# Retention followed by a feed-forward block: the later token blocks in units of 256 tokens by 4 heads, and state products as 64x64 TensorE tiles

## The chip, the cores and the metric

The kernel runs on one core of one Trainium2 chip. The metric is the device time of one execution in microseconds (us). One execution was profiled; its trace gives the start and duration of every instruction.

## The reference

Retention with a decay per head, then a two-layer feed-forward block with PReLU; all inputs and the output are float32.

```python
# q, k, v: (4, 8, 768, 64); w_in: (512, 2048); w_out: (2048, 512); alpha: (2048,)
gamma = 1.0 - 2.0 ** (-5.0 - np.arange(H))          # per head
for t in range(S):
    state = gamma[None, :, None, None] * state + np.einsum('bhd,bhe->bhde', k[:, :, t], v[:, :, t])
    y[:, :, t] = (1 / sqrt(D)) * np.einsum('bhd,bhde->bhe', q[:, :, t], state)
x = y.transpose(0, 2, 1, 3).reshape(B * S, H * D)   # (3072, 512)
h = x @ w_in
out = (np.maximum(h, 0) + alpha * np.minimum(h, 0)) @ w_out
```

## The kernel before

The 3072 tokens are six blocks of 512. A block is four units, and unit `u` runs through the same steps:

- **Load**: k, q and v come from memory through SP's queue (`load`, lines 131 and 139).
- **Scale**: k and q are multiplied by powers of gamma from a table `tab` and rounded to float16 (`kdq`; `prep` line 157 or `u_scale` line 289), v is rounded (`vx`). In blocks 2 to 5 GpSimd (POOL) does all three; in blocks 0 and 1 VectorE (DVE) does k.
- **Turn**: `kdq` is transposed into `kq`, by TensorE and a ScalarE (ACT) copy in blocks 0 and 1 (`u_turn`), by a DMA transpose on SP's queue later (line 165).
- **State**: k times v per pair of heads (`stp`), added to the carried state on VectorE (`ss`), multiplied by the decay on GpSimd (`tg`). A sequence is six chunks of 128 tokens, and the last one needs no new state.
- **Scores**: k times q (`sca`, `scb`), masked on VectorE into `m2`.
- **Output**: `yps` gathers the carried state times q and the masked scores times v; ScalarE copies it into `xT`, the input of the feed-forward block.

There are two forms of unit. Blocks 0 and 1 (units 0 to 7, functions with `u_`) take 256 tokens by 4 heads: two units share the tokens and halve the heads. Partition `p` holds two neighbouring tokens, so a load reads runs of 512 bytes. Its products use one row half of TensorE for the first 128 tokens and the other for the next (`hf`). Blocks 2 to 5 (units 8 to 23: `prep`, `stage_a`, `stage_b`, `stage_c`) take 128 tokens by 8 heads, with runs of 256 bytes.

The trace writes a product's tile shape as rows*columns of the TensorE array: `128*128` is the whole array, `64*64` one of four tiles. In blocks 2 to 5 the state (L199) and the carried product (L248) are 128*128, the product with v (L258) 128*64, the scores (L223) 64*128. In blocks 0 and 1 the state (L341) is 64*128, the scores (L381) and the product with v (L415) are 64*64, the carried product (L427) 128*128.

The feed-forward block is `ffn1(n)` (16 groups of 4 wide products, L460; ScalarE computes `hm` at L470 and VectorE `gt` at L471 from each) and `ffn2(n)` (64 wide products, L500; ScalarE copies `os` at L509 and issues the store itself at L513). Both are generators. `tick(gen, m)` issues the next `m` wide products, and the schedule written out by hand puts the short products of the next block between them. I call such an insertion a visit. In blocks 2 to 5 there are five per block: four within `ffn2` that start a unit and (from the second on) put out the one before, and a last one that only puts out.

All PSUM tiles share eight banks under one tag (`ps`). Every engine takes its instructions in the order in which the program issues them, so the hand-written order decides what waits behind what: on SP the loads and the transposes, on ScalarE the copies and the stores, on GpSimd the scaling, the decay products and the issue of the weight loads (`get_wi`, `get_wo`). The first load of unit 8 is held until the last quarter of `w_out` has arrived (`held`).

Of the kernel before, what the change touches and what calls it, by code (L numbers as in the profile page):

```python
# [10 lines left out]
F16 = mybir.dt.float16  # L11
# [7 lines left out]
def kernel(  # L19
# [10 lines left out]
    nc = tc.nc  # L30
# [16 lines left out]
    NTAB = 6 * H + NP + 16  # L47
    TU = 2 * H + NP
    tab_np = np.zeros((128, NTAB), dtype=np.float64)
    for h in range(H):  # L50
        tab_np[:, h] = g64[h] ** (127.0 - p_ar)
        tab_np[:, H + h] = scale * g64[h] ** (p_ar + 1.0 - 128.0)
    for p in range(NP):
        tab_np[0:64, 2 * H + p] = g64[2 * p] ** 128
        tab_np[64:128, 2 * H + p] = g64[2 * p + 1] ** 128
    for s in range(2):
        loc = 2.0 * (p_ar % 64) + s
        for h in range(H):
            tab_np[:, TU + H * s + h] = g64[h] ** (127.0 - loc)
            tab_np[:, TU + 2 * H + H * s + h] = scale * g64[h] ** (loc + 1.0 - 128.0)  # L60
    tab_np[0:NFT, NTAB - 16 : NTAB] = np.eye(NFT)
    tab_np = tab_np.astype(np.float32)
    mi_np = np.zeros((128, 512), dtype=np.float16)
    mi_np[:, 0:128] = p_ar[:, None] <= p_ar[None, :]
    mi_np[:, 128:256] = np.eye(128)
    half_ar = np.arange(64)
    for s in range(2):
        for t in range(2):
            keep_np = (2 * half_ar[:, None] + s) <= (2 * half_ar[None, :] + t)
            c0 = 256 + 128 * s + 64 * t  # L70
            mi_np[0:64, c0 : c0 + 64] = keep_np
            mi_np[64:128, c0 : c0 + 64] = keep_np
# [9 lines left out]
    mi = sbp.tile([128, 512], F16, tag="mi", name="mi")  # L82
    mask = mi[:, 0:128]
    ident = mi[:, 128:256]
    masku = mi[:, 256:512].rearrange("p (s i) -> p s i", s=2)
# [8 lines left out]

    NV = 8
    NPE = 8
    NUN = 8
    vext = [sbp.tile([128, NP, 3, 64], F16, tag=f"vx{i}", name=f"vx{i}") for i in range(NV)]

# [21 lines left out]
    def load(u, names="kqv"):  # L121
        b, c = divmod(u, NCH)
        t = staged.setdefault(u, {})
        for nm in names:
            src = srcs[nm]
            st = sbp.tile([128, H * D], FP, tag=f"{nm}s", bufs=8, name=f"{nm}s{u}")
            if u < NUN:
                j, g = divmod(u, 2)
                b, c = divmod(2 * j, NCH)
                t[nm] = st.rearrange("p (h s d) -> p s h d", s=2, d=D)  # L130
                ins = nc.sync.dma_start(  # L131
                    out=st.rearrange("p (h x) -> p h x", h=H // 2),
                    in_=src[
                        b, H // 2 * g : H // 2 * g + H // 2, C * c : C * c + 2 * C, :
                    ].rearrange("h (p s) d -> p h (s d)", s=2),
                )
            else:
                t[nm] = st.rearrange("p (h d) -> p h d", d=D)
                ins = nc.sync.dma_start(  # L139
                    out=t[nm],  # L140
                    in_=src[b, :, C * c : C * c + C, :].rearrange("h p d -> p h d"),
                )
# [10 lines left out]
    def prep(u):  # L153
        t = staged.pop(u)
        kdq = sbp.tile([128, 2, H, D], F16, tag="kdq", bufs=8, name=f"kdq{u}")
        for a, nm in enumerate("kq"):
            nc.gpsimd.tensor_tensor(  # L157
                out=kdq[:, a],
                in0=t[nm],
                in1=tab[:, H * a : H * a + H].unsqueeze(2).to_broadcast([128, H, D]),  # L160
                op=MULT,
            )
        kq = sbp.tile([128, 2 * NP, 128], F16, tag="kq", bufs=8, name=f"kq{u}")
        if u >= NPE:
            nc.sync.dma_start_transpose(
                out=kq, in_=kdq.rearrange("p a h d -> p (a h d)")
            )
        vx = vext[u % NV]
        nc.gpsimd.tensor_copy(  # L169
            out=vx[:, :, 0::2, :],  # L170
            in_=t["v"].rearrange("p (a b) d -> p a b d", b=2),
        )
        prepped[u] = (kdq, kq, vx)


# [3 lines left out]
    def stage_a(u):  # L179
        b, c = divmod(u, NCH)  # L180
        kdq, kq, vx = prepped.pop(u)
        kd = kdq[:, 0]
        if u < NPE:
            trb = ps("trb", F16, 1024)
            for p in range(2 * NP):
                nc.tensor.transpose(
                    out=trb[:, 128 * p : 128 * p + 128],
                    in_=kdq[:, p // NP, 2 * (p % NP) : 2 * (p % NP) + 2, :].rearrange(
                        "p a d -> p (a d)"
                    ),  # L190
                    identity=ident,
                )
            nc.scalar.activation(
                out=kq.rearrange("p a i -> p (a i)"), in_=trb, func=COPY, bias=0.0, scale=1.0
            )
        if c < NCH - 1:
            stp = ps("stp")
            for p in range(NP):
                nc.tensor.matmul(  # L199
                    out=stp[:, 128 * p : 128 * p + 128],  # L200
                    lhsT=kd[:, 2 * p : 2 * p + 2, :].rearrange("p a d -> p (a d)"),
                    rhs=vx[:, p, 0::2, :],
                    start=True,
                    stop=True,
                )
            new = sst[u % NT]
            stv = stp.rearrange("p (a e) -> p a e", e=128)
            tg = sbp.tile([128, NP, 128], F16, tag="tg", bufs=4, name=f"tg{u}")
            if c > 0:
                nc.vector.tensor_tensor(out=new, in0=tgs[u], in1=stv, op=ADD)  # L210
                nc.gpsimd.tensor_tensor(out=tg, in0=new, in1=gmat, op=MULT)  # L211
            else:
                nc.vector.tensor_tensor(out=tg, in0=stv, in1=gmat, op=MULT)
            tgs[u + 1] = tg
        live[u] = (kq.rearrange("p a i -> p (a i)"), vx)

    def stage_b(u):
        kq, vx = live[u]
        scs = [ps("sca"), ps("scb")]
        for p in range(NP):  # L220
            for lh in range(2):
                s = slice(64 * lh, 64 * lh + 64)
                nc.tensor.matmul(  # L223
                    out=scs[lh][:, 128 * p : 128 * p + 128],
                    lhsT=kq[s, 128 * p : 128 * p + 128],
                    rhs=kq[s, 512 + 128 * p : 512 + 128 * p + 128],
                    start=True,
                    stop=True,
                )
        m2s = []  # L230
        for lh in range(2):
            m2 = sbp.tile([128, NP, 128], F16, tag=f"m2{lh}", bufs=2, name=f"m2{lh}")
            nc.vector.tensor_tensor(  # L233
                out=m2,
                in0=scs[lh].rearrange("p (a i) -> p a i", i=128),
                in1=mask.unsqueeze(1).to_broadcast([128, NP, 128]),
                op=MULT,
            )
            m2s.append(m2)
        live[u] = (kq, vx, m2s)  # L240

    def stage_c(u):
        b, c = divmod(u, NCH)
        kq, vx, m2s = live.pop(u)
        yps = ps("yps")
        if c > 0:
            for p in range(NP):
                nc.tensor.matmul(  # L248
                    out=yps[:, 128 * p : 128 * p + 128],
                    lhsT=tgs[u][:, p, :],  # L250
                    rhs=kq[:, 512 + 128 * p : 512 + 128 * p + 128],
                    start=(p == 0),
                    stop=False,
                    skip_group_check=True,
                )
        for p in range(NP):
            for lh in range(2):
                nc.tensor.matmul(  # L258
                    out=yps[64 * lh : 64 * lh + 64, 128 * p : 128 * p + 128],
                    lhsT=vx[:, p, 2 * lh, :],  # L260
                    rhs=m2s[lh][:, p, :],
                    start=(c == 0 and p == 0),
                    stop=(p == NP - 1),
                    skip_group_check=True,
                )
        n, i = divmod(u, UB)
        if i == 0:
            xT[n] = sbp.tile([128, NP, TB], F16, tag="xT", bufs=2, name=f"xT{n}")
        nc.scalar.activation(  # L269
            out=xT[n][:, :, C * i : C * i + C],  # L270
            in_=yps.rearrange("p (a i) -> p a i", i=128),
            func=COPY,
            bias=0.0,
            scale=1.0,
        )


    def u_scale(i, a):
        if i not in prepped:
            kdq = sbp.tile([128, 2, H, D], F16, tag="kdq", bufs=8, name=f"kdq{i}")  # L280
            kq = sbp.tile([128, 2 * NP, 128], F16, tag="kq", bufs=8, name=f"kq{i}")
            prepped[i] = (
                kdq.rearrange("p a (s h) d -> p a s h d", s=2),
                kq,
                vext[i % NV].rearrange("p (s r) x d -> p s r x d", s=2),
            )
# [459 lines left out]
```

## Time and profile before

| | |
|---|---|
| Time, median of 3 runs (lowest to highest) | 221.58 us (221.4 to 223.0) |
| The profiled execution's own time | 221.09 us |
| Its span, first to last instruction | 219.3 us |
| Mean granted TensorE clock | 0.997 of full speed |
| TensorE busy / VectorE / ScalarE / GpSimd | 96% / 55% / 45% / 37% of the span |
| First product of `ffn1(1)`; start of its unbroken run | 56.42 us; 57.97 us |
| `ffn2` of blocks 1, 2, 3, 4 of the loop (visits for blocks 2 to 5) | from 71.5, 104.4, 136.8 and 169.0 us |
| DMA packets under 512 bytes | 67888 of 87507 |

The busy share of TensorE counts overlapping products and is no measure of its peak; the starts of its products tell more. The groups of instructions and the timeline give the line, the engine, the operation, the tile names and the shapes. `PEld` is TensorE's weight load, `SPq` and `ACTq` are the time in which SP's and ScalarE's queues issue a DMA. An entry such as `[0.30 <-DMA kq<-kdq]` is idle time ahead of an instruction and what ended it.

### The profile page before, as it was taken

What the parts mean: (1) busy time and instruction counts of PE and PEld (TensorE: products, weight loads), DVE (VectorE), ACT (ScalarE), POOL (GpSimd) and SP (SyncE); (2) the same over time, 40 slices, a digit from 0 to 9 for tenths busy, and PEclk for the clock granted to TensorE, in tenths of its full rate; (3) what the DMA queues carried; (4) which work ended last, traced back from release to release, by engine and by line L of the source; (5) the groups of instructions that cost most, each with busy time, mean ns of one, the idle gap of its engine ahead of it and who ended that gap; (6) DMA issues with size and microseconds to landing.
All of it is one profiled execution on the core that took longest, in us unless ns stands there. A gap on an engine that the chain in (4) does not pass through costs nothing.

```text
span 219.3 us, 4001 instructions
## 1 busy us (share of the span) xinstructions
PE 209.6 (96%) x1575; PEld 103.8 (47%) x1575; DVE 121.1 (55%) x190; ACT 98.5 (45%) x169; POOL 81.5 (37%) x96
## 2 busy tenths in 40 slices
PE   7899998999899999999999999999999999999992
PEld 3456543454444554444555444555444555444440
DVE  4684896554039953188753288653388742388000
ACT  2583873334359422467232476222576222566121
POOL 3487208731963249900044960205950420000000
PEclk9999999999999999999999999999999999999998
DMA  6999999958999999999911699912640102100111
GB/s 184 300 218 189 193 261 298 218 98 199 259 262 218 216 229 210 236 242 228 200 48 53 173 244 221 223 50 96 146 96 0 44 20 82 48 3 0 48 73 72
DMA packets 87507, 33.99 MB, mean 155 GB/s; under 512 B 67888, under 2 KB 84416, under 8 KB 87488
## 3 DMA queue, kind: packets, MB, share of 16 engines
q1 hardware_dynamic: 79488, 23.08, 47.4%
q0 software_dynamic: 4224, 4.19, 12.2%
q10 hardware_dynamic: 3776, 6.47, 8.0%
q8 instruction: 12, 0.20, 0.4%
q14 instruction: 7, 0.06, 0.1%
HBM read 27.44 MB, written 6.29 MB: 154 GB/s over the span
## 4 chain that ended last, share of the span: by engine, by line
PE 71%; DMA 16%; SPq 6%; POOL 2%; ACT 2%; DVE 1%; issue 1%; ACTq 0%; DVEq 0%
PE hps L460 31%; PE ops L500 31%; DMA vs<-in_v_dram 5%; SPq L131 5%; DMA qs<-in_q_dram 5%; DMA win<-in_moe_w_in_dram 3%; DMA kq<-kdq 2%; PE yps L258 2%; PE sca L223 2%; PE stp L199 1%; SPq L139 1%; PE yps L248 1%; POOL tg L364 1%; ACT kq L322 1%; DVE m L394 1%
## 5 line engine op out<-in xcount | busy, mean ns | idle before, releaser
L471 DVE SCALAR_TENSOR_TENSOR gt<-hm,oma,hps 128x512 f16<-128x512 f32 x96 | 69.3, 745 | 41.2 <-ACT hm L470 34.3
L500 PE MATMUL ops<-wout,gt 128*128 128x512 f16 x384 | 89.4, 380 | 0.0
L460 PE MATMUL hps<-xT,win 128*128 128x512 f16 (+1 forms) x404 | 84.5, 368 | 1.3 <-ACT xT L440 1.3
L470 ACT ACTIVATE hm<-hps 128x512 f32<-128x512 f32 x96 | 56.7, 597 | 22.2 <-PE hps L460 21.0
L460 PEld LDWEIGHTS <-win 128*128 128x128 f16 x404 | 39.3, 97 | 45.0 <-issue 1.8
L500 PEld LDWEIGHTS <-gt 128*128 128x128 f16 x384 | 35.1, 98 | 40.6
L211 POOL TENSOR_TENSOR tg<-ss,gmat 128x512 f16<-128x512 f32 x11 | 14.0, 1270 | 66.6 <-DVE ss L210 66.6
L509 ACT ACTIVATE os<-ops 128x512 f32<-128x512 f32 x24 | 14.3, 598 | 39.3 <-PE ops L500 31.5
L269 ACT ACTIVATE xT<-yps 128x512 f16<-128x512 f32 x16 | 9.6, 597 | 32.3 <-PE yps L258 30.9
L157 POOL TENSOR_TENSOR kdq<-ks,tab 128x512 f16<-128x512 f32 x16 | 16.8, 1049 | 1.8 <-DMA ks<-in_k_dram 1.8
L157 POOL TENSOR_TENSOR kdq<-qs,tab 128x512 f16<-128x512 f32 x16 | 16.8, 1049 | 0.8 <-DMA qs<-in_q_dram 0.8
L322 ACT ACTIVATE kq<-trb 128x512 f16<-128x512 f16 (+1 forms) x11 | 8.7, 790 | 16.0 <-PE trb L313 15.9
L233 DVE TENSOR_TENSOR m<-sca,mi 128x512 f16<-128x512 f32 x16 | 11.0, 690 | 8.6 <-PE scb L223 7.9
L210 DVE TENSOR_TENSOR ss<-tg,stp 128x512 f32<-128x512 f16 x11 | 7.5, 686 | 13.2 <-PE stp L199 13.0
L289 POOL TENSOR_TENSOR kdq<-qs,tab 128x512 f16<-128x512 f32 x8 | 8.3, 1039 | 17.3 <-DMA qs<-in_q_dram 17.3
L233 DVE TENSOR_TENSOR m<-scb,mi 128x512 f16<-128x512 f32 x16 | 10.9, 681 | 0.0
L364 POOL TENSOR_TENSOR tg<-ss,gmat 128x256 f16<-128x256 f32 x10 | 7.7, 777 | 8.3 <-DVE ss L363 8.3
L169 POOL CAST vx<-vs 128x512 f16<-128x512 f32 x16 | 9.9, 616 | 0.3 <-ACT hm L470 0.3
L111 PE MATMUL kps<-spin 128*128 128x512 f16 x22 | 8.3, 496 | 1.5 <-DVE spin L528 1.5
L394 DVE TENSOR_TENSOR m<-sca,mi 128x512 f16<-128x512 f32 x8 | 5.5, 692 | 7.2 <-PE scb L381 6.6
L440 ACT ACTIVATE xT<-yps 128x256 f16<-128x256 f32 x16 | 6.2, 453 | 5.4 <-PE yps L427 4.0
L289 DVE TENSOR_TENSOR kdq<-ks,tab 128x512 f16<-128x512 f32 x8 | 6.2, 781 | 4.3 <-DMA ks<-in_k_dram 4.3
(43 smaller groups left out, 111.5 us busy)
## 6 DMA issues: line engine op xcount, KB each, us to landing
ks<-in_k_dram SPq DMA_DIRECT2D x24, 256.0 KB, 4.4
qs<-in_q_dram SPq DMA_DIRECT2D x24, 256.0 KB, 4.5
vs<-in_v_dram SPq DMA_DIRECT2D x24, 256.0 KB, 4.9
out_dram<-os ACTq DMA_DIRECT2D x24, 256.0 KB, 2.2
win<-in_moe_w_in_dram POOLq DMA_DIRECT2D x4, 512.0 KB, 6.9
wout<-in_moe_w_out_dram POOLq DMA_DIRECT2D x4, 512.0 KB, 9.2
kq<-kdq SPq DMA_TRANSPOSE x16, 4.3
mi<-mi_const ACTq DMA_DIRECT2D x1, 128.0 KB, 2.9
```

Source lines behind the costliest of these rows:

```text
L131: ins = nc.sync.dma_start(out=st.rearrange("p (h x) -> p h x", h=H // 2), in_=src[b, H // 2 * g : H // 2 * g + H // 2, C * c : C * c + 2 * ...
L157: nc.gpsimd.tensor_tensor(out=kdq[:, a], in0=t[nm], in1=tab[:, H * a : H * a + H].unsqueeze(2).to_broadcast([128, H, D]), op=MULT,)
L169: nc.gpsimd.tensor_copy(out=vx[:, :, 0::2, :], in_=t["v"].rearrange("p (a b) d -> p a b d", b=2),)
L211: nc.gpsimd.tensor_tensor(out=tg, in0=new, in1=gmat, op=MULT)
L233: nc.vector.tensor_tensor(out=m2, in0=scs[lh].rearrange("p (a i) -> p a i", i=128), in1=mask.unsqueeze(1).to_broadcast([128, NP, 128]), op ...
L289: (nc.vector, nc.gpsimd)[a].tensor_tensor(out=prepped[i][0][:, a], in0=staged[i]["kq"[a]], in1=tab[:, o : o + 2 * H] .rearrange("p (s h) - ...
L322: nc.scalar.activation(out=kq.rearrange("p a i -> p (a i)")[:, c0:c1], in_=trb[:, c0:c1], func=COPY, bias=0.0, scale=1.0,)
L460: nc.tensor.matmul(out=hpss[ft][:, lo:hi], lhsT=w_in_all[:, hp, 128 * ft : 128 * ft + 128], rhs=xT[n][:, hp, lo:hi], start=(hp == 0), stop ...
L470: nc.scalar.activation(out=hm, in_=hpt, func=RELU, bias=0.0, scale=-1.0)
L471: nc.vector.scalar_tensor_tensor(out=gt[:, ft, :], in0=hm, scalar=oma_sb[:, ft : ft + 1], in1=hpt, op0=MULT, op1=ADD,)
L500: nc.tensor.matmul(out=opss[tq], lhsT=gt[:, ft, 128 * tq : 128 * tq + 128], rhs=w_out_all[:, ft, :], start=(ft == 0), stop=(ft == NFT - 1),)
L509: nc.scalar.activation(out=os_sb, in_=opss[tq], func=COPY, bias=0.0, scale=1.0)
```

## The change

Units 8 to 23 are now computed by the `u_` functions too, so `prep`, `stage_a`, `stage_b` and `stage_c` are gone and every load reads runs of 512 bytes. In blocks 2 to 5 GpSimd still scales k and q and rounds v, and the DMA transpose stays (`u_flip`). The state products of all units are 64*64 tiles: twice as many products as with 64*128, each for one head's rows of the state instead of two. The products with v alternate the row halves innermost, and from block 2 on the carried product comes ahead of them instead of behind. In block 1 the state no longer has a visit of its own behind the turn: `u_begin` and `u_mid` become `u_turn` and `u_visit`, which issues state and scores together. `vx` becomes a dense tile of its own for each unit, without the zeroed middle part, whose eight memsets on VectorE go. Two constant tables shrink.

The core of the diff (the tables and removed functions left out):

```diff
-                for hf in halves:
-                    z = slice(64 * hf, 64 * hf + 64)
-                    nc.tensor.matmul(
-                        out=stps[hf][:, 128 * r : 128 * r + 128],
-                        lhsT=kdu[z, 0, s, 2 * r : 2 * r + 2, :].rearrange("p a d -> p (a d)"),
-                        rhs=vx[z, s, r, 0::2, :],
-                        start=(s == 0),
-                        stop=(s == 1),
-                    )
+                for lh in range(2):
+                    for hf in halves:
+                        z = slice(64 * hf, 64 * hf + 64)
+                        nc.tensor.matmul(
+                            out=stps[hf][64 * lh : 64 * lh + 64, 128 * r : 128 * r + 128],
+                            lhsT=kdu[z, 0, s, 2 * r + lh, :],
+                            rhs=vx[z, 2 * r : 2 * r + 2, s, :],
+                            start=(s == 0),
+                            stop=(s == 1),
+                            skip_group_check=True,
+                        )
...
+    def u_flip(i):
+        kdu, kq, vx = prepped[i]
+        nc.sync.dma_start_transpose(
+            out=kq, in_=kdu.rearrange("p a s h d -> p (a s h d)")
+        )
...
+        def carried(first):
+            for hf in range(2):
+                z = slice(64 * hf, 64 * hf + 64)
+                for r in range(2):
+                    if inter[hf]:
                         nc.tensor.matmul(
+                            out=ypss[hf][:, 128 * r : 128 * r + 128],
                             lhsT=tgs[2 * j + hf][:, 2 * g + r, :],
                             rhs=kqv[:, 1, :, r, z],
...
+        def own(first):
             for r in range(2):
+                for s in range(2):
+                    for lh in range(2):
+                        for hf in range(2):
+                            z = slice(64 * hf, 64 * hf + 64)
+                            nc.tensor.matmul(
+                                out=ypss[hf][64 * lh : 64 * lh + 64, 128 * r : 128 * r + 128],
+                                lhsT=vx[z, 2 * r + lh, s, :],
+                                rhs=m2s[lh][z, s, r, :],
...
+        if i < 2 * UB:
+            own(True)
+            carried(False)
+        else:
+            carried(True)
+            own(False)
...
-    def u_begin(i):
-        u_turn(i, (0, 1))
+    def u_visit(i):
         st[i] = u_state(i)
+        m[i] = u_scores(i)
         st[i](0)
-
-    def u_mid(i):
-        m[i] = u_scores(i)
         masked(i)
         st[i](1)
...
     tick(gen, 4)
-    u_begin(4)
+    u_turn(4, (0, 1))
     tick(gen, 6)
-    u_mid(4)
+    u_visit(4)
     u_prep(5)
     held.append(get_wo(3))
     tick(gen, 8)
-    u_begin(5)
+    u_turn(5, (0, 1))
     u_prep(6)
     tick(gen, 2)
     u_out(4)
     tick(gen, 4)
-    u_mid(5)
+    u_visit(5)
...
             for i in range(UB):
                 tick(gen, 14)
-                prep(u0 + i)
+                u_prep(u0 + i, nc.gpsimd)
+                u_flip(u0 + i)
                 if u0 + i + UB < NU:
                     load(u0 + i + UB)
...
                 tick(gen, 2)
-                stage_a(u)
                 if i:
-                    stage_c(u - 1)
-                stage_b(u)
+                    u_out(u - 1)
+                u_visit(u)
                 tick(gen, 12)
-            stage_c(u0 + UB - 1)
+            u_out(u0 + UB - 1)
```

## The prediction

> **What bounds the kernel now.** I read the page's busy rows first, then the chain of waits in order of time, then TensorE's timeline inside one visit, then ScalarE's around the end of block 0's second product.
>
> ```profile
> PE 209.6 (96%) x1575; PEld 103.8 (47%) x1575; DVE 121.1 (55%) x190; ACT 98.5 (45%) x169; POOL 81.5 (37%) x96
> ```
> ```profile
> 57.97 13.74 PE hps L460 x65
> 71.71 0.43 PE ops L500 x2
> ...
> 80.29 4.93 DMA kq<-kdq
> ...
> 187.79 13.81 PE hps L460 x64
> 201.60 13.83 PE ops L500 x64
> 215.45 0.60 ACT os L509
> ```
> TensorE is busy 96%, and from 57.97 us the chain is TensorE alone, but for one transpose (kq). 64 wide products take 13.81 us, 0.216 each, and the change leaves them alone. What it can alter there is the visits, the short products between L500's. One of them:
>
> ```profile
> 112.55 0.39 PE L199 MATMUL stp<-vx,kdq 128*128 128x128 f16 x4
> 112.78 0.39 PE L248 MATMUL yps<-kq,tg 128*128 128x128 f16 x4
> 113.09 0.41 PE L258 MATMUL yps<-m,vx 128*64 128x128 f16 x8
> 113.44 0.23 PE L223 MATMUL sca<-kq 64*128 64x128 f16 x1
> ...
> 113.77 0.60 PE L500 MATMUL ops<-wout,gt 128*128 128x512 f16 x2
> ```
> Read the starts, not the durations: products overlap. L199 to L248 is four products in 0.224, 0.056 each; I call that a slot. L248 to L258 is 0.31 for four again: the change of tile shape (128*128 to 128*64) adds 0.09. L258 to L223 is 0.35 and L223 to L500 0.33, each four slots of pairs that run side by side, plus a change of shape. The visit takes 1.216, with three such changes.
>
> ```profile
> 41.33 0.42 PE L415 MATMUL yps<-m,vx 64*64 64x128 f16 x16
> 41.68 0.40 PE L427 MATMUL yps<-kq,tg 128*128 128x128 f16 x4
> ```
> Sixteen 64*64 products take 0.35 up to the next shape: four slots of four tiles (0.224), a slow first slot (0.02), the change (0.09).
>
> **Visits of blocks 2 to 5.** Work in slots stays equal: before 4 state, 4 carried, 4 with v, 4 scores; after 4 carried (128*128), then 16 products with v, 16 of the state, 16 scores, all 64*64, so 12 slots in one shape. Such a visit is 4 x 0.056 + 0.093 to enter + 0.35 + 8 x 0.056 = 1.115, against 1.216: one change of shape less. The first visit of a block becomes 0.093 + 0.35 + 0.224 = 0.667 (before 0.648), its last output 0.667 (0.664). Against that, the old code skips L199 for a sequence's last chunk (3 of 16 units, 12 slots). The new one skips only one row half in six units, whose 8 products still take 4 slots as pairs. That costs 12 x 0.056 = 0.67. Where the carried product of a sequence's first chunk falls away, both save the same 8 products.
>
> Summed over the 20 visits by the timeline's starts, before: 5.19, 4.74, 4.52, 4.74 in blocks 2 to 5 (19.18). After, by the formula: 4.68, 4.46, 4.46, 4.68 (18.27). The difference is 0.91: **0.46** from shapes net of the extra slots, and **0.45** from two waits in block 2. One is 0.37 for the transposed kq at 85.27; the other 0.09 at 76.3, where the second mask ends 76.26.
>
> The kq wait goes because the loads of 512-byte runs are shorter: the 12 loads at L131 from 26.63 took 10.7 us, the 12 at L139 from 48.34 took 15.4. The queue of SP is gapless from there to the fourth transpose (80.29), so that one is issued some 3 us earlier or more. The mask wait goes because VectorE's add ahead of the masks shrinks from 0.68 (L210) to 0.42 (L363).
>
> [...]
>
> What else the visits move is covered. VectorE per visit: 0.42 + 0.69 + 0.68 + 0.42 = 2.2 within 14 wide products, 3.02. POOL's two tg at 0.72 against one at 1.27: free until the next visit. ScalarE's two xT copies (0.76 for both, against 0.60) behind the last output: 8 wide products, 1.73, follow before FFN1 reads them. Without that cover, each 0.1 would go straight on the end. A visit takes six banks instead of four. The allocator hands out the bank whose last reader is oldest, so the nearest reuse is a mask or copy of the visit before, 3 us old.
>
> **Block 1 (35 to 58 us).** u_begin and u_mid become u_turn and u_visit. A unit before: state 0.096 + 0.33 + 0.01, scores 0.093 + 0.35 + 0.01, together 0.88. After: 0.093 + 0.35 + 0.224 + 0.01 = 0.68. Four units: -0.82. The bank wait in u_out (0.46 at 46.15 where 0.42 is normal, twice) goes too: -0.08.
>
> But the state of unit 4 now comes after the six wide products, so its tg on POOL moves from 36.79 to about 38.0, and everything behind it on POOL's queue with it: q of unit 5 (1.03) to 38.75-39.78, the cast of v, the issue of wout's last quarter (39.02 to about 40.8). On VectorE k of unit 5 starts near 39.1, now while POOL multiplies. Before, that happened once:
>
> ```profile
> 33.58 1.03 POOL L289 TENSOR_TENSOR kdq<-qs,tab 128x512 f16<-128x512 f32 x1 [10.46 <-DMA qs<-in_q_dram]
> 33.74 1.43 DVE L289 TENSOR_TENSOR kdq<-ks,tab 128x512 f16<-128x512 f32 x1
> ...
> 39.17 0.68 DVE L289 TENSOR_TENSOR kdq<-ks,tab 128x512 f16<-128x512 f32 x1
> ```
> VectorE's multiply took 1.43 instead of 0.68, ending 0.56 behind POOL's. So kdq of unit 5 ends near 40.35 and u_turn(5), which TensorE already waits for at 39.91, starts 40.4: +0.5, and unit 4's 0.2 is lost in it. Left are 3 x 0.2 + 0.08 - 0.5 = 0.2 earlier at FFN1(1)'s first product (56.42).
>
> What opens FFN1(1) is not TensorE but ScalarE's queue:
>
> ```profile
> 53.46 0.60 ACT L509 ACTIVATE os<-ops 128x512 f32<-128x512 f32 x1 [1.24 <-PE ops L500]
> 54.97 0.36 ACTq L513 DMA_DIRECT2D out_dram<-os  x1
> 55.38 0.60 ACT L509 ACTIVATE os<-ops 128x512 f32<-128x512 f32 x1 [1.32 <-PE yps L427]
> 56.77 0.34 ACTq L513 DMA_DIRECT2D out_dram<-os  x1
> 57.16 0.76 ACT L440 ACTIVATE xT<-yps 128x256 f16<-128x256 f32 x2 [1.19 <-DMA qs<-in_q_dram]
> 57.77 0.60 ACT L509 ACTIVATE os<-ops 128x512 f32<-128x512 f32 x1
> ```
> The copies end 54.06 and 55.98, their stores are issued 0.91 and 0.79 later, each as a load of SP (L139) ends. Behind the second waits xT of unit 7, and behind that TensorE, 1.06 at 57.97. The next two stores wait 2.6 and 0.8, so FFN1(1)'s hm begins only at 63.21. With loads of 0.9 instead of 1.28 us I take those waits down by the same share and a little more: 1.7 to about 1.1 ahead of xT. With the 0.2 that is **-0.8** (not over -1.0: TensorE itself arrives near 57.0), and FFN1(1)'s short bank wait at 64.34 (0.08) goes: -0.85. The loads start up to 1.3 later, since the first is held for wout's last quarter (48.3 now). Bounds: 0, if the later loads press on the same two stores as much; -1.8, if no wait is left and VectorE isn't held up.
>
> The front (0 to 35 us) I put at nothing. Its steps wait for loads, POOL and ScalarE; the removed memsets of vx end at 2.56, before k arrives (3.78). The end behind 201 is unchanged.
>
> **Sum.** 221.09 (the profiled run; its span 219.3) - 0.46 - 0.45 - 0.85 = 219.3. The median of the runs shown, 221.58, lies 0.5 above that run, so I say **219.8**, own range 219.2 to 220.6.
>
> **Rivals.**
> A, more than that: no wait on ScalarE's stores, VectorE isn't held. FFN1(1) opens at 56.2: -1.8, with 0.91: 218.9. For it: the transfer time falls by 30%. Against: SP still loads without a pause there.
>
> B, nothing gained ahead of FFN1(1): the later loads delay the stores as before. 221.58 - 0.91 = 220.7. For it: such waits vary from 0.8 to 2.6.
>
> C, the other side: TensorE can't be fed. A visit now holds 52 products, each with its weight load, where it held 24. If the queue passes a pair every r us and about 16 pairs are ahead when the visit begins (the longest full-speed burst shown), 36 must pass in 1.115: it decides from r = 0.031. The rows show bursts of 16 at 0.013 (L381, 10.18 to 10.38, behind a wait), but sustained only 0.053: 38 products from 44.74 to 46.77. At the middle, 0.042, a visit takes 1.51, 12 x 0.4 = 4.8 more: 224.6. At 0.053 it would be 229. [...] Against C: the burst at 10.18 follows a wait, and full speed right behind it speaks for quick issue.
>
> D, the change doesn't do what it says for the half units: their 8 products on one row half run singly, 0.22 more in eight units: 221.5. Against: the four tiles of L415 start 3 ns apart, two of them on the same rows.
>
> **Chances.** Forecast 0.42, A 0.20, B 0.20, C 0.12, D 0.06. About 1%, 2.2 us, is what a measurement of this kernel can tell from no change. Faster by more (under 219.4): A 0.17, the forecast's lower part 0.13: 0.30. Slower (over 223.8): C 0.10 and 0.02 for unseen mishaps. The rest, 0.58, lies between. The range runs from 218.2 (A with a little more) to 223.2 (B, D and the lower end of C).
>
> **What would show it.** Right: a visit at 1.11 to 1.13 from the first carried product to L500, twelve slots of 0.056 with no gap; no wait on kq in block 2; FFN1(1) opening near 57.1; a kdq multiply of 1.2 or more for unit 5. Wrong: spread starts late in a visit (C), half units 0.2 longer (D), u_turn(5) before 40.0, or the store waits as long as now (B).

## The result and the profile after

The changed kernel takes 222.62 us (median of 20 executions, 220.69 to 225.72), the kernel before 221.08 (20, 220.24 to 223.92). The ratio is 1.0057, 95% interval 1.0030 to 1.0083: slower by 0.6%, where 219.8 was forecast. The ratios here leave out executions over 1.5% longer than the fastest of the same kernel, so they are not always the quotient of the two medians. The profiled execution after took 222.42 us, span 220.6 (before: 221.09 and 219.3), granted clock 0.996.

The busy row and the chain of waits after. Columns of the chain: start, length, what.

```profile
PE 209.0 (95%) x2043; PEld 104.3 (47%) x2043; DVE 119.6 (54%) x195; ACT 100.9 (46%) x185; POOL 83.1 (38%) x107
```
```profile
58.58 6.13 DMA vs<-in_v_dram
...
64.79 0.34 ACTq L388
...
66.66 7.07 PE hps L335 x32
```

TensorE has 468 products more and is busy 0.6 us less, yet the span grew by 1.3. The chain before was TensorE alone from 57.97 on, but for one transpose; now it runs through a load of SP, ScalarE's store (L388) and only then, at 66.66, through TensorE. So the time was lost ahead of that. A visit of block 3, on TensorE's timeline:

```profile
110.28 0.28 PE L280 MATMUL yps<-kq,tg 128*128 128x128 f16 x2
110.49 0.42 PE L295 MATMUL yps<-m,vx 64*64 64x128 f16 x16
110.74 0.39 PE L204 MATMUL stp<-vx,kdq 64*64 64x128 f16 x16
110.96 0.22 PE L245 MATMUL sca<-kq 64*64 64x128 f16 x1
...
111.29 3.20 PE L375 MATMUL ops<-wout,gt 128*128 128x512 f16 x14
```

From L280 to L375 it is 1.00 with two carried products (1.11 with four, in the other visits): slots of 0.056 and a single change of shape, as the formula has it. From the first product of one `ffn2` to the first of the next `ffn1`, blocks 2 to 5 shrank by 0.28, 0.29, 0.08 and 0.07, together 0.72. The loss is ScalarE's, around the end of block 0's second product:

```profile
53.95 0.60 ACT L384 ACTIVATE os<-ops 128x512 f32<-128x512 f32 x1 [1.29 <-PE ops L375]
56.41 0.36 ACTq L388 DMA_DIRECT2D out_dram<-os  x1
56.82 0.60 ACT L384 ACTIVATE os<-ops 128x512 f32<-128x512 f32 x1 [2.28 <-DMA qs<-in_q_dram]
58.56 0.41 ACTq L388 DMA_DIRECT2D out_dram<-os  x1
59.02 0.76 ACT L315 ACTIVATE xT<-yps 128x256 f16<-128x256 f32 x2 [1.59 <-DMA vs<-in_v_dram]
```

The copies end at 54.55 and 57.42, their stores are issued 1.86 and 1.14 later (before 0.91 and 0.79), xT of unit 7 is copied at 59.02, and FFN1(1), which began at 56.91, runs unbroken only from 59.83 (57.97). The account up to the first product of ffn2(1) (71.54 before, 73.57 after): u_turn(5) 1.20 later, -0.71 from there to FFN1(1)'s first product, +1.37 at the stores, +0.17 in a bank wait: +2.03. With -0.72 this is the 1.3 of the span.

One row of the front gave the lead to the rest. DMA activity between 10.5 and 12.3 us, when only loads of units 2 and 3 run, by the same code in both kernels (columns: packets, MB, their time as a share of 16 engines). Before:

```profile
q1 hardware_dynamic: 1062, 0.53, 101.1%
```

After:

```profile
q1 hardware_dynamic: 1054, 0.52, 122.6%
```

A packet of 512 bytes took 1.011 x 16 x 1.8 us / 1062 = 27 ns before and 33.5 ns after. The number of packets is the same: with a share of 122.6% they overlap more, so this row shows longer packets and not fewer bytes. For these loads the two programs differ in the address that they write to. The two constant tables lost 64 and 256 bytes per partition, 320 together, and every tile allocated behind them moved (the room that `vx` gave up is a multiple of 512): in the program before, the weights, the staged k, q and v, `kdq` and `kq` all start on a multiple of 512, in the program after 192 bytes past one.

### The profile page after: what moved, and what is told of

The parts are those of the page before. It is cut to its first block, busy times and chain, and to the rows that moved or that the text cites. A ratio compares the mean times of both kernels' runs of the same rounds, so it can differ in the third digit from the quotient of the medians.

```text
span 220.6 us, 4964 instructions
## 1 busy us (share of the span) xinstructions
PE 209.0 (95%) x2043; PEld 104.3 (47%) x2043; DVE 119.6 (54%) x195; ACT 100.9 (46%) x185; POOL 83.1 (38%) x107
## 3 DMA queue, kind: packets, MB, share of 16 engines
q0 software_dynamic: 4224, 4.19, 12.3%
## 4 chain that ended last, share of the span: by engine, by line
PE 73%; DMA 12%; POOL 4%; SPq 3%; DVE 3%; issue 2%; ACT 1%; ACTq 0%; POOLq 0%; DVEq 0%
PE ops L375 35%; PE hps L335 28%; DMA qs<-in_q_dram 5%; DMA win<-in_moe_w_in_dram 4%; SPq L118 3%; PE yps L295 3%; DMA vs<-in_v_dram 3%; PE stp L204 2%; POOL tg L228 2%; POOL kdq L145 2%; PE yps L280 2%; PE sca L245 1%; DVE m L258 1%; POOL win L418 1%; PE scb L245 1%
## 5 line engine op out<-in xcount | busy, mean ns | idle before, releaser
L346 DVE SCALAR_TENSOR_TENSOR gt<-hm,oma,hps 128x512 f16<-128x512 f32 x96 | 69.1, 745 | 41.5 <-ACT hm L345 34.9
L375 PE MATMUL ops<-wout,gt 128*128 128x512 f16 x384 | 89.3, 380 | 0.0
L345 ACT ACTIVATE hm<-hps 128x512 f32<-128x512 f32 x96 | 56.5, 597 | 24.3 <-PE hps L335 21.9
L228 POOL TENSOR_TENSOR tg<-ss,gmat 128x256 f16<-128x256 f32 x32 | 23.2, 727 | 82.4 <-DVE ss L227 82.4
L375 PEld LDWEIGHTS <-gt 128*128 128x128 f16 x384 | 35.3, 98 | 39.9
L315 ACT ACTIVATE xT<-yps 128x256 f16<-128x256 f32 x48 | 18.5, 453 | 35.2 <-PE yps L295 28.4
L227 DVE TENSOR_TENSOR ss<-tg,stp 128x256 f32<-128x256 f16 x32 | 13.2, 415 | 25.2 <-PE stp L204 25.2
L258 DVE TENSOR_TENSOR m<-scb,mi 128x512 f16<-128x512 f32 x24 | 16.3, 680 | 0.0
L161 POOL CAST vx<-vs 128x512 f16<-128x512 f32 x20 | 12.7, 635 | 0.0
L204 PE MATMUL stp<-vx,kdq 64*64 64x128 f16 x320 | 9.7, 219 | 0.4 <-ACT vx L159 0.4
L295 PE MATMUL yps<-m,vx 64*64 64x128 f16 x384 | 10.0, 222 | 0.0
L245 PE MATMUL sca<-kq 64*64 64x128 f16 x192 | 9.7, 217 | 0.2
L245 PE MATMUL scb<-kq 64*64 64x128 f16 x192 | 9.7, 219 | 0.0
L223 DVE TENSOR_TENSOR tg<-stp,gmat 128x256 f16<-128x256 f32 x8 | 3.4, 423 | 11.0 <-PE stp L204 11.0
```

Source lines behind the costliest of these rows:

```text
L204: nc.tensor.matmul(out=stps[hf][64 * lh : 64 * lh + 64, 128 * r : 128 * r + 128], lhsT=kdu[z, 0, s, 2 * r + lh, :], rhs=vx[z, 2 * r : 2 * ...
L228: nc.gpsimd.tensor_tensor(out=tgs[u + 1][:, gs, :], in0=new, in1=gmat[:, gs, :], op=MULT)
L245: nc.tensor.matmul(out=scs[lh][z, c0 : c0 + 128], lhsT=kqv[y, 0, s, r, z], rhs=kqv[y, 1, :, r, z], start=True, stop=True,)
L258: nc.vector.tensor_tensor(out=m2, in0=scs[lh].rearrange("p (s r i) -> p s r i", s=2, r=2), in1=masku.unsqueeze(2).to_broadcast([128, 2, 2, ...
L295: nc.tensor.matmul(out=ypss[hf][64 * lh : 64 * lh + 64, 128 * r : 128 * r + 128], lhsT=vx[z, 2 * r + lh, s, :], rhs=m2s[lh][z, s, r, :], s ...
L315: nc.scalar.activation(out=xT[n][:, 2 * g : 2 * g + 2, c0 : c0 + C].rearrange("p a (i s) -> p a s i", s=2), in_=ypss[hf][:, 0:256].rearran ...
```

## The experiments

Ratios are to the kernel before, run beside each on the same chip, with their 95% intervals.

**The order in block 1, and the stores' place (e1 to e4).** At first I took the order in block 1 for the cause, and a crowd at the stores for the rival.

e1_order: after, with the old order in block 1.

```diff
-    u_turn(4, (0, 1))
+    u_begin(4)          # turn and state
     tick(gen, 6)
-    u_visit(4)
+    u_mid(4)            # scores; units 5 to 7 likewise
```

> The changed kernel with the old order in block 1 (the state of units 4 to 7 directly behind the turn again), all else as changed. Theory 1, the loss is made by block 1's new order (unit 4's decay product late on GpSimd, so the last quarter of w_out is issued some 2.4 us later, so block 2's loads fall on ScalarE's stores): w_out's last quarter is issued near 39.4 again, u_turn(5) near 40.3, ffn1(1) runs unbroken from about 58.0, and the kernel is 0.8 us faster than the one before, near 220.3. Rival 2, the loads of 512 bytes crowd the stores whatever the order: ffn1(1) opens at 59 or later and the kernel stays 1 us slower than before. Rival 3, the loss comes from the first 35 us (weights landing 1.4 us later): unit 4's turn starts near 36.1 as in the changed kernel, ffn1(1) opens about 58.9, time within 0.3 us of before.

Measured: 222.22 us, ratio 1.0084 [1.0057, 1.0112]. Undoing the order gains nothing; it is not the cause.

e2_stores and e3_before_stores: block 0's four stores are kept and issued one after each 14 wide products of FFN1(1), in the kernel after and in the kernel before.

```diff
-                        nc.scalar.dma_start(out=out[row : row + 128, :], in_=os_sb)
+                        kept.append((row, os_sb))      # block 0 only
...
                 tick(gen, 14)
+                if kept: nc.scalar.dma_start(...)      # the oldest one
```

> The changed kernel with the four stores of block 0's output issued one by one during ffn1(1) instead of between the copies of ffn2(0). All theories that put the loss on ScalarE's queue: ffn1(1) opens by TensorE's own arrival, near 57.6 instead of 59.8, no bank wait near 66, and the time falls by 2.2 to 2.7 us against the changed kernel, to about 220.1, 1.1 under the kernel before. If the opening of ffn1(1) had another cause (a late xT for want of TensorE or GpSimd), it stays near 59.8 and the time does too.

> The kernel before with the same four stores moved. If stores also gate it, ffn1(1) opens near 57.0 instead of 58.0 and the bank wait at 64.3 goes: about 1.0 us faster than before, 220.1. The difference to the changed kernel with moved stores is then the change's own worth without that queue: by my sum the visits of blocks 2 to 5 give 0.9 and block 1's slower turn takes about 0.5 away, so the two should lie 0.4 apart or less.

Measured: 222.57, ratio 1.0107 [1.0059, 1.0156], and 219.66, ratio 0.9980 [0.9944, 1.0016]. After the move FFN1(1) opens without a gap in both. In the changed kernel the stores now stand in `hm`'s way instead, and block 2's visits fill with waits (e2's profiled execution, 225.99 us, is the longest of its six; e8 below shows the same in another); in the kernel before they don't. Moving them is no cure, and it didn't name the cause.

e4_pool: after, with unit 5's q and the last quarter of `w_out` ahead of unit 4's visit on GpSimd.

> The changed kernel with GpSimd's order mended in block 1: q of unit 5 and the issue of w_out's last quarter come ahead of unit 4's visit. Theory 1: the last quarter is issued near 38.5 instead of 41.5, block 2's loads start near 46.5 instead of 49.0, u_turn(5) starts near 40.5 instead of 41.1, ScalarE's first two stores wait less than 1 us each again and ffn1(1) opens near 57.5: about 2 us faster than the changed kernel. Rival 2 (512-byte loads crowd the stores whenever they run): the stores still wait 1 to 2 us each and ffn1(1) opens after 58.8.

Measured: 223.12, ratio 1.0121 [1.0079, 1.0163]: nothing gained. But the front showed a pattern: the last wide product ahead of u_turn(4) starts at 34.1 to 34.9 in e1, e2 and e4, in whichever order block 1 is, and at 33.5 in e3 (before 33.75, after 34.09). Something that all kernels with the small tables share seemed late there, and that led to the packets. The lead was luck: by the later runs this start doesn't tell the tables apart. It is 34.55 in e8 and 34.62 in e12, whose tiles are aligned, and 33.64 in e13, whose tiles are not.

**The address (e5 to e8).**

e5_pad320, e7_pad64: after, with an unused tile ahead of the weights. e6_before_pad192: the kernel before, so shifted.

```diff
+    sbp.tile([128, 80], FP, tag="pad", name="pad")     # e7: 16, e6: 48
     w_in_all = sbp.tile([128, 4, d_ff], F16, tag="win", name="win")
```

> The kernel after with an unused tile of 320 bytes per partition allocated ahead of the weights; nothing else is changed. The two constant tables that the change shrank (272 to 208 bytes and 1024 to 768) moved every later tile by 320 bytes, so the weights, the staged k, q and v, kdq and kq start 192 bytes past a multiple of 512, where in the kernel before they start on one. The pad puts them back on multiples of 512. In the four traces of the kernel after and its variants a back-to-back load of k, q or v at L118 moves its 512-byte packets in 34 ns each (12 loads from 8 us on), in the two traces of the kernel before the same loads take 27. Theory ADDRESS: a packet of 512 bytes that straddles a multiple of 512 in the destination takes 34 ns, and this is where the front's +0.33 and the longer waits of ScalarE's stores come from. Then: packets back at 27 ns, last L375 product ahead of u_turn(4) near 33.75 (after: 34.09), first held load near 26.7 (after: 28.0), FFN1(1) unbroken from 57.2 to 58.0 (after: 59.83), time 219.3 to 220.6, ratio to the kernel before 0.992 to 0.998. Rival CROWD: the 512-byte loads of block 2 crowd the stores whatever their addresses, and 34 ns has another cause: packets at 34 ns still, or at 27 with FFN1(1) opening near 59.5 all the same; 222.2 to 222.6, ratio 1.005.

> The kernel before with an unused tile of 192 bytes per partition ahead of the weights, so that all later tiles start 192 bytes past a multiple of 512, as in the kernel after. Theory ADDRESS: the loads of blocks 0 and 1 (512-byte packets) go from 27 to 34 ns, the front ends 0.3 later (last L500 product ahead of u_turn(4) near 34.1 instead of 33.75), the first held load near 28 instead of 26.6, unit 4's and 5's turns 0.5 to 1 later; the 256-byte packets of blocks 2 to 5 from 18 to some 20 to 24; FFN1(1) opens 1 to 2 later than 57.97; time 222 to 223.5, ratio 1.004 to 1.012. Rival CROWD: nothing but the address is changed, so 27 ns, 33.75, 57.97 and 221.1, ratio 0.998 to 1.002.

> The kernel after with an unused tile of 64 bytes ahead of the weights, so that the later tiles start 256 bytes past a multiple of 512. One look at the packets. If what counts is the multiple of 512, the back-to-back 512-byte packets of L118 still take 34 ns, the time is 222 to 223. If multiples of 256 are enough, 27 ns and the times of the run with the pad of 320 (219.3 to 220.6). If addresses play no part, 34 ns in both.

Measured: e5 220.47 us, ratio 0.9951 [0.9922, 0.9980]; e6 222.52, ratio 1.0063 [1.0034, 1.0092]; e7 219.86 in its one execution. The same window of DMA activity in e5:

```profile
q1 hardware_dynamic: 1053, 0.52, 101.4%
```

And in e6:

```profile
q1 hardware_dynamic: 1060, 0.53, 113.6%
```

e5 has 27.7 ns, e6 30.9 there (33.5 in its loads of block 1), e7 26.7. An unused tile makes the changed kernel 1.06% faster, 2.3 us, from slower than before to faster than before; another makes the kernel before 0.63%, 1.4 us, slower (uncertain by 0.4% and 0.3%). That the shift of the tiles costs time is shown, in both directions. It moves all tiles from the weights on, and which of them cost the time is not separated. By e7 a start on a multiple of 256 is enough for the packets; its time is one execution. Not all the signs expected in the traces came. In e5's profiled execution (221.79 us, 1.3 above its median) the first held load starts at 27.80 (26.7 expected, 28.00 after) and FFN1(1) runs unbroken only from 59.69 (57.2 to 58.0 expected); in e6 the 256-byte packets of block 2's loads take 18.6 ns (20 to 24 expected). Why a start at 192 makes a packet longer is not shown; in these loads it is the destination that was moved.

e8_pad320_stores: e5 and e2 together.

> The kernel after with the pad of 320 bytes, and with block 0's four output stores issued one after each stretch of 14 wide products in FFN1(1), as in the run e2_stores (222.57 without the pad, with waits in all visits of block 2) and e3_before_stores (the kernel before so changed: 219.66). Theory ADDRESS: the long waits of e2's stores came from the slower packets, so FFN1(1) opens without a gap near 56.6 and block 2's visits have no wait: 218.3 to 219.3, the fastest of all. Rival CROWD: the moved stores collide with the 512-byte loads and transposes as in e2: 222.0 to 223.

Measured: 222.28, ratio 1.0026 [0.9994, 1.0057]. The expectation failed: packets at 27 ns, FFN1(1) without a gap, and yet ScalarE's stores wait among the `hm` (the second 2.4), and block 2's `ffn2` takes 22.6 instead of 18.8. The waits of e2 do not come from the address. What a store waits for is told below (ScalarE's stores): one earlier DMA's landing. Counted from unit 8's first load, e8's four stores wait 0.76, 2.43, 2.57 and 1.26 us for the 10th, 14th, 16th and 19th load; e3's wait 0.63, 0.51, 1.88 and 0.15 for the 7th, the 10th, a transpose and the 14th.

**The stores (e9, e10, e12).** e5's FFN1(1) still ran unbroken only from 59.7, its first two stores waited 2.49 and 0.77, with packets as fast as before.

e9_loads_held: e5, with the loads of units 9 to 11 held until block 0's last output copy.

```diff
     for u in range(2 * UB, 3 * UB):
+        if u == 2 * UB + 1:
+            held.append(osc[0])        # the last copy into os
         load(u)
```

> The kernel after with the pad of 320 bytes, and with the nine loads of units 9 to 11 held until block 0's last output copy; unit 8's three go as before. In e5_pad320 the packets are fast again, but ScalarE's first two stores still waited 2.5 and 0.8, so the step of the prediction that shrank these waits along with the packets gave nothing. Theory CROWD (now for what is left): a store waits behind the loads that SP has already issued; without them ScalarE's first two stores wait under 0.5, FFN1(1) runs unbroken from near 56.8 (e5_pad320: 59.7, e7_pad64: 57.8), and unless a transpose comes too late for block 2 (unit 8's stands in SP's queue behind load 11, near 64.5) the time is 218.4 to 219.8, ratio 0.987 to 0.993. Rival: the wait belongs to the store itself and not to the loads ahead of it: waits of 0.8 and more, 220.5, ratio 0.995.

Measured: 219.47, ratio 0.9947 [0.9918, 0.9976]. ScalarE's timeline in e9:

```profile
53.54 0.60 ACT L387 ACTIVATE os<-ops 128x512 f32<-128x512 f32 x1 [1.29 <-PE ops L378]
54.16 0.36 ACTq L391 DMA_DIRECT2D out_dram<-os  x1
54.57 0.60 ACT L387 ACTIVATE os<-ops 128x512 f32<-128x512 f32 x1 [0.44 <-PE ops L378]
55.20 0.34 ACTq L391 DMA_DIRECT2D out_dram<-os  x1
```

With the nine loads held, the stores go 0.02 after their copies and FFN1(1) runs from 56.5: the wait is for loads, and not the store's own. The time is no better than e5's, though e10 below shows 1.5 us to be had there: 0.8 of it is seen to go to a late transpose (a visit of block 2 waits that long for kq), the rest is within the intervals.

e10_pool_stores and e12_before_pool_stores: block 0's stores are issued by GpSimd, in e5 and in the kernel before.

```diff
-                        nc.scalar.dma_start(out=out[row : row + 128, :], in_=os_sb)
+                        (nc.scalar if n else nc.gpsimd).dma_start(out=out[row : row + 128, :], in_=os_sb)
```

> The kernel after with the pad of 320 bytes, and with block 0's four output stores issued by GpSimd instead of ScalarE (GpSimd's queue has nothing but the scaling of units 8 to 11 there; its issues take 0.8 each). If what opens FFN1(1) is ScalarE standing at its stores, as the prediction has it, xT of unit 7 is copied right behind its product, FFN1(1) runs unbroken from 56.0 to 56.9, hm begins near 57.5, and the time is 217.8 to 219.3, ratio 0.984 to 0.991. If something else holds FFN1(1), nothing gained: 220.5, ratio 0.995. If GpSimd waits at the stores as ScalarE does, unit 8's kdq ends 3 or more later and the first visits of block 2 wait for kq: 221 or more.

> The kernel before with block 0's four output stores issued by GpSimd. Here ScalarE's stores cost 1.55 ahead of FFN1(1) by the profile (57.97 instead of 56.42) and the chain then goes on TensorE alone. If ScalarE's queue is what opens FFN1(1): 56.4, time 219.4 to 220.2, ratio 0.992 to 0.996. The difference to e10_pool_stores then shows the change without the addresses and without the stores: 0.46 and 0.45 (or less, where the earlier transposes take away the wait for kq) from the visits and 0.2 from block 1, in all 0.6 to 1.1. If the stores are hidden anyway: 221.2.

Measured: e10 217.69 us, ratio 0.9883 [0.9856, 0.9910], the best but for e14, which ties; e12 219.59, ratio 0.9970 [0.9945, 0.9994]. The chain of e10 is TensorE alone again:

```profile
55.89 13.82 PE hps L336 x68
69.71 0.43 PE ops L376 x2
```

So ScalarE at its stores is what opens FFN1(1). It costs the aligned change about 0.7% (e5 to e10, 1.5 us, uncertain by 0.4%), the kernel before 0.3%. With addresses and stores both out of the way the change is worth 0.9883 / 0.9970, some 0.9% or 1.9 us, each ratio uncertain by 0.3%. Expected were 0.6 to 1.1 us, and the traces show 1.05 (0.96 in the visits, 0.09 in block 1); the times don't tell this from 1.9.

**The shape (e11).**

```diff
-                for lh in range(2):
-                    for hf in halves:
...
+                for hf in halves:
+                    z = slice(64 * hf, 64 * hf + 64)
+                    nc.tensor.matmul(
+                        out=stps[hf][:, 128 * r : 128 * r + 128],
+                        lhsT=kdu[z, 0, s, 2 * r : 2 * r + 2, :].rearrange("p a d -> p (a d)"),
```

> The kernel after with the pad of 320 bytes, and with the state products as 64x128 tiles again (8 per unit with 128 rows of output instead of 16 with 64), the rest as after. By the formula of the prediction the slots stay equal (8 products as pairs on the two row halves are 4 slots of 0.056), but the tile shape changes twice more in a visit, at 0.09 each: 1.30 instead of 1.115, 16 visits: +2.9, so 223.0 to 224.0, ratio to the kernel before 1.007 to 1.013. If a change of shape between tiles that use one row half costs less (0.02, as at a first slot), +0.3 to +0.6: 220.8 to 221.2, ratio 0.996 to 0.999.

Measured: 224.13, ratio 1.0159 [1.0109, 1.0209], 2% over e5. A visit on TensorE's timeline:

```profile
109.72 0.28 PE L279 MATMUL yps<-kq,tg 128*128 128x128 f16 x2
109.92 0.42 PE L294 MATMUL yps<-m,vx 64*64 64x128 f16 x16
110.27 0.40 PE L204 MATMUL stp<-vx,kdq 64*128 64x128 f16 x8
110.60 0.24 PE L244 MATMUL sca<-kq 64*64 64x128 f16 x1
...
110.95 3.19 PE L374 MATMUL ops<-wout,gt 128*128 128x512 f16 x14
```

1.23 against 1.00 for the same visit with 64*64 (full visits 1.34 against 1.11): two changes of shape at 0.115, a little over the 0.09 of the prediction. Eight products fewer are 0.23 slower, because they have another shape. Twelve visits at 0.23 and eight at 0.10 that put out nothing (the first of blocks 2 to 5 and the four of block 1) are 3.6 us, 1.6%.

**What was left (e13, e14).** e13_pool_stores_nopad is e10 without the pad. e14_q5_early is e10 with unit 5's q on GpSimd ahead of unit 4's visit.

```diff
     tick(gen, 6)
+    u_scale(5, 1)
     u_visit(4)
-    u_prep(5)
+    u_scale(5, 0)
+    u_cast(5)
```

> The kernel after without the pad (tiles 192 bytes past a multiple of 512, packets of 34 ns) and with block 0's four stores issued by GpSimd: e10_pool_stores (217.69, ratio 0.988) but for the addresses. It tells by which way the slow packets cost 2.3 us (e5_pad320 against the kernel after). Theory STORES: nearly all by the stores that stand behind more slow packets. Then with the stores out of the way FFN1(1) runs unbroken from 56.0 to 56.5, and the time is 217.7 to 218.5, ratio 0.988 to 0.992. Theory FRONT: by later loads of weights and of units 2 to 6 in the first 45 us (the front ends 0.3 later and unit 4's and 5's turns 0.5 to 1.2 later in the traces with 34 ns), so that they stay: 218.9 to 219.9, ratio 0.993 to 0.998, FFN1(1) from 56.6 to 57.2.

> The kernel e10_pool_stores (pad of 320 bytes, stores of block 0 on GpSimd) with the scaling of q of unit 5 on GpSimd ahead of unit 4's visit instead of behind it, so that GpSimd works on it while TensorE runs the six wide products ahead of the visit. The prediction put +0.5 on this place: unit 4's decay product on GpSimd comes later, q of unit 5 behind it, and VectorE multiplies k of unit 5 while GpSimd multiplies q, at 1.2 or more instead of 0.68. e10's trace has TensorE waiting 1.28 there (0.53 in the kernel before). If that is the cause, k of unit 5 takes 0.68 again, the gap ahead of u_turn(5) falls to some 0.55 and the time by 0.5 to 0.8: 216.9 to 217.3, ratio 0.984 to 0.987. If the wait is for something else (the load of unit 5, the last quarter of w_out): 217.7, ratio 0.988.

Measured: e13 218.94, ratio 0.9923 [0.9896, 0.9950]; e14 217.69, ratio 0.9868 [0.9820, 0.9916]. Between e10 and e13 lies 0.4%, 0.9 us, uncertain by as much. A single cost of some 0.7% lies within the intervals of e5 against after, of e6 and of this pair, so how much of the address's cost goes through the stores, if any, can't be told from the times. The traces show none of it there: ahead of xT the first two stores wait 3.0, 1.2 and 2.4 us together with shifted tiles (after, e1, e4), 3.3, 2.1 and 2.5 without (e5, e7, e11), and in the kernel before 1.6 shifted (e6) and 1.7 not. FFN1(1) opens at 56.04 in e13, as theory STORES had it, while the time is nearer to FRONT's. Where the address's cost falls stays open. In e14 TensorE's pause ahead of u_turn(5) falls from 1.28 to 0.82 and unit 5's k from 1.25 to 0.79, but the expected gain of 0.5 to 0.8 us doesn't show: the time can't be told from e10's.

## Why the prediction was wrong, point by point

**Visits: right.** 1.11 for a full one, 0.667 for the last output, no late spread of the starts (C) and no longer visits for the half units (D: 1.11 as well). Where the stores don't disturb it (e10), blocks 2 to 5 are 0.53, 0.29, 0.07 and 0.07 shorter than in the profile before, 0.96 for a forecast of 0.91. In the changed kernel itself 0.24 comes back as a wait in block 2's first visit. The transposed kq no longer keeps TensorE waiting (idle 0.30 ahead of 85.27 in the profile before; in the profile after no idle time of TensorE over 0.15 ends with a kq). The state in 64*64 tiles does not slow the visits by its weight loads: in the profile after these take 106 ns each (L204), L415's in the profile before 105 and the state's with 128*128 tiles (L199) 98, and e11, with wider tiles for the state, is slower.

**Block 1: right in its parts.** From u_turn(5) to FFN1(1)'s first product 0.71 was saved (3 x 0.2 + 0.08 forecast), and the collision on unit 5 came as described:

```profile
39.47 1.03 POOL L145 TENSOR_TENSOR kdq<-qs,tab 128x512 f16<-128x512 f32 x1
...
39.81 2.27 DVE L145 TENSOR_TENSOR kdq<-ks,tab 128x512 f16<-128x512 f32 x2
```

Two multiplies in a row, the first (unit 5) 1.25 long. e14 separates them and gets back 0.46 of pause: the +0.5 had the right size. Net, from the first product behind u_turn(4) to FFN1(1)'s first it is 20.55 (after, e5, e7 and e10 alike) instead of 20.64: 0.1 gained, not 0.2.

**ScalarE's stores: the step that failed.** "I take those waits down by the same share and a little more: 1.7 to about 1.1" was worked out from the length of a load. Measured ahead of xT: 3.0, and still 3.3 (e5) and 2.1 (e7) with fast packets. The prediction saw that each wait ends with a load, but not which load sets it, and that, not a load's length, is what changed. For each DMA the trace lists the semaphore (a counter) that its landing raises. As this program is built, the DMAs of SP and ScalarE share eight semaphores, and ahead of 23 of the 24 stores stands an instruction that waits for the store's own semaphore; for the four stores of block 0 it ends 0.04 us after the last DMA with that semaphore has landed, before and after. Before, the first two stores take over the semaphores of the third and the fifth load of block 2, which land at 54.89 and 56.69. The chain of waits before has the second:

```profile
52.20 4.49 DMA qs<-in_q_dram
56.77 0.34 ACTq L513
...
57.16 0.77 ACT xT L440 x2
```

After, they take over those of the fifth and the sixth load, which land at 56.34 and 58.48, and the fourth store that of the twelfth:

```profile
58.58 6.13 DMA vs<-in_v_dram
...
64.73 0.02 ACTq L388
...
64.79 0.34 ACTq L388
```

In every run that leaves them on ScalarE, each store of block 0 that waits over 0.1 us is issued within 0.1 us of the landing of its semaphore's last user. The loads did get faster: the fifth lands 7.29 us after the first one's issue instead of 8.35. But in the changed program the stores are tied to later loads. The third load lands at 54.57 there, as the first copy ends (54.55), so tied to it the first store would hardly have waited; that is worked out from the landings and not run. In e9 the semaphores were last used by loads landed by 44.85, and in e10 GpSimd's stores have others, last used by weights landed by 26.25: no such wait in either. Why the build ties the stores to other loads in the changed program is not shown. Rival B named the outcome (nothing gained ahead of FFN1(1), 220.7), and e5 is that case, 220.47.

**"The front I put at nothing", and "two constant tables shrink": the second.** The prediction has no term for the tables. Their effect is on every address behind them, 2.3 us by e5, more than all the terms of the sum (1.8), and 1.4 by e6. Of the 1.2 by which u_turn(5) came later, 0.6 arises between u_turn(4) and it, for the 0.5 forecast, and 0.6 ahead. That 0.6 can't be laid to the addresses by one trace: in e12, whose front is the kernel before's, the first product behind u_turn(4) is 0.8 late.

**The sum.** -0.9 (visits) stands and -0.2 (block 1) is -0.1; the -0.6 of the stores is +1.4 in the profile after, and with fast packets +1.6 in e5's and +0.5 in e7's; the addresses add 1.4 to 2.3, and where they do stays open. The forecast's ratio, 219.8 / 221.58 = 0.992, lies just outside what the aligned change (e5) shows, 0.9951 [0.9922, 0.9980]: even there the stores' term failed.

## What to carry to other kernels

A tile that shrinks moves all that are allocated behind it: work out the new addresses, keep tiles that DMAs fill on multiples of 256 bytes, as here (a packet took 26.7 to 27.7 ns there and 33.5 at 192 past), and compare the packets' own times before looking for a cause in the order of the work. Where a store is issued by an engine whose next copy opens a product, look up whose landing its issue waits for: issuing four of them from another engine (e10) was worth 1.5 us. Count a stretch of small products by its slots and its changes of shape (here 0.056 and 0.09 to 0.115 us), not by its products.

## What was unexpected of the hardware

A start 192 bytes past a multiple of 256 made a 512-byte packet take 33.5 ns instead of 27; the changed kernel's loads that were not back to back still showed 27.5 (29 to 32 us). In e8, after 3 us of broken work around 71 to 74 us, eight wide products came 0.427 apart instead of 0.216 (granted clock 0.62 and 0.52 in the two stretches from 74 to 78 us), though 2.4 us of idle time in FFN1(1) of the changed kernel left the clock at 1.00.
